# Sigmoid attention and FFN: float32 scores of unsplit q and k in the first three batches, and a decode without GpSimd

## The chip, the cores and the metric

The kernel runs on one core of one Trainium2 chip. The metric is the device time of one execution in microseconds; lower is better. The engines are named as in the profile: PE is TensorE (matmuls), PEld its weight loads, DVE is VectorE, ACT is ScalarE, POOL is GpSimd, SP is the queue that issues most DMAs.

## The reference

Two parts follow each other. Attention with a sigmoid in the place of the softmax, for 8 batches, 12 heads, 448 positions and a head dimension of 64, all float32:

```
scores = scale * np.matmul(q, k.transpose(0, 1, 3, 2)) - np.log(S)
attn = 1.0 / (1.0 + np.exp(-scores))
return np.matmul(attn, v).astype(np.float32)
```

Then a feed-forward network over the 3584 tokens (d_model 768, d_ff 2048). Its weights come as float64:

```
h = x @ w_in
g = 0.5 * h * (1.0 + erf(h * inv_sqrt2))
return (g @ w_out).astype(np.float32)
```

## The kernel before

**The split.** Most matmuls take operands of type `float32r`, which drop low bits. To keep the precision, an operand is split: ACT casts it to float32r (the high part), DVE subtracts that from the original (the low part), and PE sums three products, low by high, high by low, high by high. In FFN1 and FFN2 these are L450 to L452 and L497 to L499; each has 512 moving columns.

**Decoding.** `decoder()` (L92) turns the weights' float64 words into float32, once, in chunks of at most 384 columns (68 chunks; a unit is a block of w_in of 768 columns or of w_out of 1024). The chunk's raw words are loaded by SP (L118). `start` runs three DVE passes (L125 masks the exponent, L126 and L129 put the mantissa's bits together). `convert` runs two ACT passes over the exponent (L137, L140) and makes the mantissa a float32, on DVE (L142), or on ACT for chunks 24 to 39 (L146). `end` adds the sign on DVE (L154), and POOL multiplies mantissa and exponent (L163). The three steps of one chunk lie one step apart each. `decode(n)` (L187) advances this to step n; the calls are written out by hand between the other work, with the paces `PACE_A` and `PACE_F`: 20 steps in the first stage, 23 in FFN1 of block 0, the rest in the window behind it. Decoded units are stored to DRAM (scr_in by SP, scr_out by POOL's queue), and later blocks load them from there.

**Preparing.** `prepare_to` (L225) splits a unit for the matmuls: a cast on ACT (L237) and a subtraction on DVE (L238) into a tile `whl`. In block 0 there are two such tiles, so the cast for unit u+2 waits until PE is done with unit u. 

**Batches and blocks.** There are 8 batches and 7 FFN blocks of 512 tokens: a block has a batch's 448 tokens and 64 of the batch that was computed first (its results pass through DRAM, `scr_x`). The first three batches are "plain": the attention weights and v aren't split, and their product is a float32 matmul (`values_plain`, L364): 448 columns, with the two heads of a pair on the two halves of the array's columns (`pav[rows(j)]`), four chunks of keys, so eight matmuls a pair. Each float32 matmul shows as two records in the trace. For the fourth chunk of 64 keys both heads read rows 64 to 127.

The scores of all batches use split operands. `split_head` (L285) makes for each head `qs` (high part of q on the head's 64 rows, low part on the other 64; L292, L293), `ka` (cast of k, which the host has put on both row halves; L295, and a small subtraction L296) and `kb` (low part of k; L300). `scores` (L311) runs two matmuls for each chunk of 128 keys (L331, L332) and, in plain batches, two for the last 64 keys (L323, L324), and then three sigmoids on ACT (L355): 2 x 448 columns, 448 columns, and 448 on 64 rows. Behind the values, L373 (ACT) and L374 (DVE) split the result x; in the first batch SP stores it.

**The order of the work** is the order in which the code issues it, engine by engine (a manual schedule). `attention_first` (L410) computes two plain batches head by head. Then for each block `ffn1` and `window`; the window interleaves FFN2's matmuls with the attention of batch t+2, in equal shares. The third plain batch is in the window of block 0. PSUM: one score tile of two banks, four banks for values and single scores, two for the FFN.

Of the kernel before, what the change touches and what calls it, by code (L numbers as in the profile page):

```python
# [22 lines left out]
def tile_sigmoid_attention_gelu_ffn(  # L23
# [19 lines left out]
    CHUNKS = (0, 0), (1, 0), (1, 1), (0, 1)  # L43
# [14 lines left out]
    ps_f = ctx.enter_context(tc.tile_pool(name="ps_f", bufs=2, space=bass.MemoryType.PSUM))  # L58
# [17 lines left out]
    RING = 3  # L76
    PACE_A, PACE_F = 20, 23
    SUB = 384
    RAW = (("raw", RING), ("a", 2)), (("raw", RING), ("a", 2), ("ah", 3))
    EARLY, AHEAD = PACE_A + PACE_F - 3, 4  # L80
    WST = 3
    SHIFT, KEPT = 1, 4
    AHD = 3
    MLO, MHI = 24, 40
# [7 lines left out]
    def decoder():  # L92
# [3 lines left out]
            (kind, u, c0, min(SUB, width(kind) - c0))  # L96
            for kind, u in UNITS
            for c0 in range(0, width(kind), SUB)
        ]
        raws, parts, ended = {}, {}, [0]  # L100
        raw_ring = sb.tile([P, RING, 2 * SUB], U32, tag="raw", name="raw_ring", bufs=1)
        raw_next = itertools.cycle(range(RING))
        me_ring = sb.tile([P, RING, 2, SUB], U32, tag="me", name="me_ring", bufs=1)
        rings = [
            itertools.cycle([tag for n in range(4) for tag in ring if n < tag[1]]) for ring in RAW
        ]

        def load_to(n):
            for i in range(len(raws) + ended[0], min(n, len(chunks))):
                kind, u, c0, w = chunks[i]  # L110
                src = (w_in if kind == "in" else w_out)[u].rearrange("p a b -> p (a b)")
                tag, bufs = next(rings[i < EARLY])
                if tag == "raw":
                    raw = raw_ring[:, next(raw_next)]
                else:
                    raw = sb.tile([P, 2 * SUB], U32, tag=tag, name=f"raw{i}", bufs=bufs)
                raw = raw[:, : 2 * w]
                nc.sync.dma_start(raw.bitcast(I64), src[:, c0 : c0 + w])  # L118
                raws[i] = raw.rearrange("p (n t) -> p n t", t=2)

        def start(i):
            w = chunks[i][3]
            low, high = raws[i][:, :, 0], raws[i][:, :, 1]
            m, e = me_ring[:, i % RING, 0, :w], me_ring[:, i % RING, 1, :w]
            nc.vector.tensor_scalar(e, high, 0x7FF00000, None, op0=ALU.bitwise_and)  # L125
# [3 lines left out]
            nc.vector.scalar_tensor_tensor(  # L129
                m, low, 20, m, op0=ALU.logical_shift_right, op1=ALU.bitwise_or  # L130
            )
            parts[i] = m, e

        def convert(i):

            m, e = parts[i]
            nc.scalar.activation(  # L137
                e.bitcast(F32), e.bitcast(I32), AF.Relu, bias=1151.0 * 2**23, scale=-8.0
            )
            nc.scalar.activation(e, e.bitcast(F32), AF.Relu, bias=255.0 * 2**23, scale=-1.0)  # L140
            if not MLO <= i < MHI:
                nc.vector.tensor_scalar(  # L142
                    m.bitcast(F32), m.bitcast(I32), 2.0**-32, 1.5, op0=ALU.mult, op1=ALU.add
                )
            else:
                nc.scalar.activation(  # L146
                    m.bitcast(F32), m.bitcast(I32), AF.Identity, bias=1.5, scale=2.0**-32
                )

        def end(i):  # L150
            high = raws.pop(i)[:, :, 1]
            ended[0] += 1
# [10 lines left out]
            nc.gpsimd.tensor_tensor(t, m.bitcast(F32), e.bitcast(F32), op=ALU.mult)  # L163
# [12 lines left out]

    class Weights:
# [9 lines left out]
        def decode(self, n):  # L187

            while self.steps < n:
# [18 lines left out]
        def load_to(self, n):  # L208

            while self.loaded < min(n, len(self.units)):  # L210
                i = self.loaded
                b, kind, u = self.units[i]
                while self.decoded < min(i + 1, len(UNITS)):
                    self.decode(self.steps + 1)
# [45 lines left out]
    def load_pair(b, hp):  # L260
        b, h = there(b, 2 * hp)
        hp = h // 2
# [5 lines left out]
        if b == 0 and hp == 0:  # L268
            for j in range(2):
                nc.sync.dma_start(kr[:, j], k[(b - 1) % B, hp, :, j])  # L270
        else:
            nc.sync.dma_start(kr, k[(b - 1) % B, hp])
        raws[b, hp] = qr, kr

    def load_v(b, hp):
        b, h = there(b, 2 * hp)
        hp = h // 2
        if b >= B or hp >= NPAIR:
            return
        tag = ("vr", "vs")[hp % 2] if b < PLAIN else "vr"  # L280
        vr = sb.tile([P, 2, 4, D], F32, tag=tag, name=f"vr{b}_{hp}")
# [3 lines left out]
    def split_head(b, h):  # L285
        b, h = there(b, h)
        if b >= B or h >= NH:
# [3 lines left out]
        qs = sb.tile([P, S], F32R, tag="qs", name=f"qs{b}_{h}", bufs=3)  # L291
        nc.scalar.copy(qs[rows(j)], qr[rows(j)])  # L292
        nc.vector.tensor_tensor(qs[rows(1 - j)], qr[rows(j)], qs[rows(j)], op=ALU.subtract)  # L293
        ka = sb.tile([P, S + TAIL], F32R, tag="ka", name=f"ka{b}_{h}", bufs=3)
        nc.scalar.copy(ka[:, :S], kr[:, j])  # L295
# [15 lines left out]
    def scores(b, h):  # L311
        plain = b < PLAIN
        qs, ka, kb = heads.pop((b, h))
        a = []
        for t in range(2):
            tag = ("al", ("wst", "wst", "ah")[b])[t] if plain else "a"
            bufs = {"wst": WST, "a": 2}.get(tag, 3)
            a.append(sb.tile([P, 2, S], F32, tag=tag, name=f"a{b}_{h}_{t}", bufs=bufs))
# [3 lines left out]
        if plain:  # L322
            nc.tensor.matmul(last[:D], ka[:, S - TAIL : S], qs, start=True, stop=False)  # L323
            nc.tensor.matmul(last[:D], ka[:, S:], qs, start=False, stop=True)  # L324
        else:

            nc.tensor.matmul(last, ka[:, S - TAIL :], qs, start=True, stop=True)
        for c in range(3):
            keys = slice(c * P, c * P + P)
            o = sc0 if c == 0 else sc1[:, c - 1]  # L330
            nc.tensor.matmul(o, ka[:, keys], qs, start=True, stop=False)  # L331
            nc.tensor.matmul(o, kb[:, keys], qs, start=False, stop=True)  # L332
        tail = a[0][D:, 1]
        if not plain:
            nc.scalar.copy(tail, last[:D])
            nc.vector.tensor_tensor(tail, last[D:], tail, op=ALU.add)
# [243 lines left out]
```

## Time and profile before

| | us |
|---|---|
| median of 3 runs | 1276.54 (1274.54 to 1277.57) |
| the profiled execution | 1277.24 |
| its span in the trace | 1275.5 |
| first FFN1 matmul of block 0 | 112.3 |
| first FFN2 matmul of block 0 | 195.7 |
| first FFN1 matmul of block 1 | 315.95 |

The page gives busy time and idle time by engine and by group of instructions. A group's row has the line of the code, the engine, the operation, the tiles (out<-in) with their shapes, the count, then busy us and mean ns of one, then the idle time of the engine just before them and what ended it. Matmuls are pipelined: a record lasts longer than the step from one to the next, so PE's pace is read from start to start. A window's row has the length and each engine's busy time (with the count of instructions), the granted clock, the DMA share and GB/s.

### The profile page before, as it was taken

To read this page: it belongs to the slowest core of one execution; us is meant where nothing else is said; L and a number is where in the kernel's file an instruction comes from. 1 tells how busy PE (TensorE), PEld (TensorE's weight loads), DVE (VectorE), ACT (ScalarE), POOL (GpSimd) and SP (SyncE) were. 2 spreads that over 40 slices of the span, in tenths; PEclk is the share of its full clock that TensorE was granted. 3 is DMA by queue.
4 is the path that set the end of the run, shared out by engine and by line. 5 is a ranking of instruction groups with operands and counts; after the bars stand their busy time and mean duration, and the time that the engine had idled before them with its cause. 6 is when DMAs were issued, how large, how long until landed. Compare 5 with 4: busy or idle time off the path is not lost.

```text
span 1275.5 us, 15676 instructions
## 1 busy us (share of the span) xinstructions
PE 1229.8 (96%) x5448; PEld 985.9 (77%) x5448; DVE 826.7 (65%) x1359; ACT 872.2 (68%) x1427; POOL 89.1 (7%) x84
## 2 busy tenths in 40 slices
PE   7889888989999999999999999999999999999998
PEld 4445665756888888888888888888888888888887
DVE  5776888883458973479844798436985458863420
ACT  7987677764459984499844898547995469964421
POOL 1111333441000000000000000000000000000000
PEclk9999898999999999999999999999999999999999
DMA  7764756652445323554225442254422444323330
GB/s 284 233 213 127 219 185 191 204 183 88 153 143 168 113 67 102 164 158 149 66 84 167 155 143 70 91 159 150 151 75 82 156 154 139 109 66 99 116 123 34
DMA packets 83775, 176.41 MB, mean 138 GB/s; under 512 B 24432, under 2 KB 37744, under 8 KB 83696
## 3 DMA queue, kind: packets, MB, share of 16 engines
q1 hardware_dynamic: 81968, 169.12, 41.8%
q0 software_dynamic: 1728, 6.29, 1.2%
q8 instruction: 43, 0.70, 0.2%
q14 instruction: 36, 0.29, 0.1%
HBM read 149.03 MB, written 26.35 MB: 137 GB/s over the span
## 4 chain that ended last, share of the span: by engine, by line
PE 80%; DVE 7%; ACT 5%; DMA 2%; issue 2%; POOL 2%; SPq 0%; DVEq 0%; POOLq 0%; ACTq 0%
PE po L497 11%; PE po L498 11%; PE po L499 11%; PE ph L450 10%; PE ph L451 10%; PE ph L452 10%; PE pav L398 7%; PE sc L331 4%; PE sc L332 4%; ACT a L355 2%; PE pav L364 2%; POOL w_out L163 2%; DVE me_ring L154 1%; DVE whl L238 1%; DMA scr_in<-w_in 1%
## 5 line engine op out<-in xcount | busy, mean ns | idle before, releaser
L450 PE MATMUL ph<-xh,whl 128*128 128x512 f32 x672 | 263.9, 393 | 10.3 <-DVE whl L238 10.3
L497 PE MATMUL po<-g,whl 128*128 128x512 f32 x672 | 264.0, 393 | 9.5 <-DVE whl L238 9.5
L498 PE MATMUL po<-g,whl 128*128 128x512 f32 x672 | 262.9, 391 | 0.0
L499 PE MATMUL po<-g,whl 128*128 128x512 f32 x672 | 262.8, 391 | 0.0
L451 PE MATMUL ph<-xl,whl 128*128 128x512 f32 x672 | 262.8, 391 | 0.0
L452 PE MATMUL ph<-xh,whl 128*128 128x512 f32 x672 | 262.6, 391 | 0.0
L238 DVE TENSOR_TENSOR whl<-wst,whl 128x768 fp32r<-128x768 f32 (+1 forms) x168 | 179.5, 1072 | 66.8 <-ACT whl L237 63.6
L467 DVE TENSOR_TENSOR g<-gf,g 128x512 fp32r<-128x512 f32 x112 | 77.8, 695 | 213.2 <-ACT g L466 213.2
L465 ACT ACTIVATE gf<-ph 128x512 f32<-128x512 f32 x112 | 66.8, 597 | 205.1 <-PE ph L452 190.9
L450 PEld LDWEIGHTS ph<-xh,whl 128*128 128x128 f32 x672 | 126.9, 189 | 40.3 <-DVE whl L238 13.3
L237 ACT CAST whl<-wst 128x768 fp32r<-128x768 f32 (+1 forms) x168 | 155.4, 928 | 2.2 <-PE po L499 0.8
L497 PEld LDWEIGHTS po<-g,whl 128*128 128x128 f32 x672 | 126.6, 188 | 38.8 <-DVE whl L238 11.6
L355 ACT ACTIVATE a<-sc 128x896 f32<-128x896 f32 x192 | 129.6, 728 | 28.3 <-PE sc L332 24.0
L499 PEld LDWEIGHTS po<-g,whl 128*128 128x128 f32 x672 | 126.6, 188 | 27.1
L452 PEld LDWEIGHTS ph<-xh,whl 128*128 128x128 f32 x672 | 127.0, 189 | 26.6
L451 PEld LDWEIGHTS ph<-xl,whl 128*128 128x128 f32 x672 | 127.0, 189 | 26.2
L498 PEld LDWEIGHTS po<-g,whl 128*128 128x128 f32 x672 | 126.6, 188 | 23.8
L331 PE MATMUL sc<-qs,ka 128*128 128x448 f32 x288 | 108.6, 377 | 14.9 <-ACT a L355 13.6
L348 DVE TENSOR_TENSOR al<-a,ah 128x896 fp32r<-128x896 f32 x120 | 97.8, 854 | 34.8 <-ACT ah L347 34.8
L332 PE MATMUL sc<-qs,kb 128*128 128x448 f32 x288 | 107.4, 373 | 0.0
L293 DVE TENSOR_TENSOR qs<-qr,qs 64x448 fp32r<-64x448 f32 x96 | 62.0, 646 | 45.8 <-ACT qs L292 43.9
L347 ACT CAST ah<-a 128x896 fp32r<-128x896 f32 x120 | 85.6, 753 | 6.1 <-PE pav L398 4.6
(62 smaller groups left out, 1514.6 us busy)
## 6 DMA issues: line engine op xcount, KB each, us to landing
wst<-scr_in SPq DMA_DIRECT2D x96, 384.0 KB, 3.1
wst<-scr_out SPq DMA_DIRECT2D x72, 512.0 KB, 3.2
kr<-k_dram SPq DMA_DIRECT2D x47, 448.0 KB, 4.4
vr<-v_dram SPq DMA_DIRECT2D x48, 256.0 KB, 3.9
qr<-q_dram SPq DMA_DIRECT2D x48, 224.0 KB, 3.2
out_dram<-ob SPq DMA_DIRECT2D x42, 224.0 KB, 2.0
raw<-w_in_dram SPq DMA_DIRECT2D x20, 384.0 KB, 4.2
scr_in<-w_in SPq DMA_DIRECT2D x16, 384.0 KB, 4.3
```

Of the source, the lines that this page charges most:

```text
L237: nc.scalar.copy(hl[:, 0, :w], t[:, :w])
L238: nc.vector.tensor_tensor(hl[:, 1, :w], t[:, :w], hl[:, 0, :w], op=ALU.subtract)
L331: nc.tensor.matmul(o, ka[:, keys], qs, start=True, stop=False)
L332: nc.tensor.matmul(o, kb[:, keys], qs, start=False, stop=True)
L348: nc.vector.tensor_tensor(al[t][:, c], a[t][:, c], ah[t][:, c], op=ALU.subtract)
L355: nc.scalar.activation(a, sc, AF.Sigmoid, bias=NEG_LOG_S, scale=SCALE)
L450: nc.tensor.matmul(ph, wl, xh[:, cc], start=cc == 0, stop=False)
L451: nc.tensor.matmul(ph, wh, xl[:, cc], start=False, stop=False)
L452: nc.tensor.matmul(ph, wh, xh[:, cc], start=False, stop=cc == NC - 1)
L497: nc.tensor.matmul(po, wl, g[fc][:, 0], start=first, stop=False)
L498: nc.tensor.matmul(po, wh, g[fc][:, 1], start=False, stop=False)
L499: nc.tensor.matmul(po, wh, g[fc][:, 0], start=False, stop=last)
```

## The change

The first part concerns the scores of the three plain batches. q and k are no longer split: for each pair of heads and chunk of keys there are two float32 matmuls of 64 rows, head 0 on rows 0 to 63 and head 1 on rows 64 to 127. They write to two banks of one tile, and one sigmoid takes both (2 x 448 columns). For the last 64 keys the two heads write the two partition halves of one bank, and one sigmoid takes both on 128 rows. In the values of that chunk head 0 now reads rows 0 to 63. The work goes pair by pair and chunk by chunk, loads come three pairs ahead, and k is loaded for each head on its half only. During the first stage a second score tile of two banks exists; the FFN's banks are allotted behind that stage.

```diff
+    def scores_plain(n, c):
+        qr, kr, _ = raws[n]
+        keys = slice(c * P, min(c * P + P, S))
+        if c < 3:
+            pool = next(score_pools)
+            sc = pool.tile([P, 2, 512], F32, tag="sc", name=f"sc{n}_{c}")[:, :, :S]
...
+        for j in range(2):
+            o = sc[:, j] if c < 3 else sc[rows(j)]
+            nc.tensor.matmul(o, kr[rows(j), keys], qr[rows(j)], start=True, stop=True)
+        sigmoid(a, sc)
...
+    def values_plain(n):
+        for c in range(4):
+            a = attn.pop((n, c))
             for j in range(2):
-                r = slice(0, P) if c < 3 else slice(D, P)
+                r = slice(0, P) if c < 3 else rows(j)
                 nc.tensor.matmul(
-                    pav[rows(j), :S], vr[r, j, c], a[j][t][r, n], start=c == 0, stop=c == 3
+                    pav[rows(j), :S], vr[r, j, c], a[:, j] if c < 3 else a[r],
+                    start=c == 0, stop=c == 3,
                 )
...
     def attention_first():
+        total = 2 * NPAIR
+        load_plain(0)
+        load_plain(1)
+        W.decode(0)
+        load_plain(2)
+        for n in range(total):
+            for c in range(4):
+                scores_plain(n, c)
+                if c == 1 and n > 0:
+                    values_plain(n - 1)
+                W.decode(PACE_A * (4 * n + c + 1) / (4 * total))
+            load_plain(n + 3)
+            if n == NPAIR + 2:
                 load_tokens(0)
+            W.prepare_to(min(n - total + 3, 2))
+        values_plain(total - 1)
```

The second part is the decode. Chunks are a whole unit of w_in (768 columns) or half a unit of w_out (512), 40 in all. The mantissa stays an integer, and the last DVE pass scales it and multiplies it by the exponent; L142, L146 and POOL's L163 are gone. A chunk takes two steps: three DVE passes; then the two ACT passes, and behind them the last two DVE passes of the chunk before and the load of the chunk after next. The paces are 14 chunks in the first stage, 8 in FFN1 of block 0 and up to 22 in the window. Three raw buffers and two pairs of mantissa and exponent remain.

```diff
-    PACE_A, PACE_F = 20, 23
-    SUB = 384
+    PACE_A, PACE_F, PACE_W = 14, 8, 22
+    SUB_IN, SUB_OUT = NC * P, NFH * P // 2
...
             nc.vector.tensor_scalar(
-                m, high, 12, 0x80000000, op0=ALU.logical_shift_left, op1=ALU.bitwise_xor
+                m, high, 11, 0x80000000, op0=ALU.logical_shift_left, op1=ALU.bitwise_or
             )
             nc.vector.scalar_tensor_tensor(
-                m, low, 20, m, op0=ALU.logical_shift_right, op1=ALU.bitwise_or
+                m, low, 21, m, op0=ALU.logical_shift_right, op1=ALU.bitwise_or
             )
...
-            nc.gpsimd.tensor_tensor(t, m.bitcast(F32), e.bitcast(F32), op=ALU.mult)
+            nc.vector.scalar_tensor_tensor(
+                t, m, 2.0**-31, e.bitcast(F32), op0=ALU.mult, op1=ALU.mult
+            )
...
+        for i in range(len(chunks) + 1):
+            if i == 0:
+                load(2)
             if i < len(chunks):
                 start(i)
+                yield False
+                scale(i)
+            if i > 0:
+                end(i - 1)
+                load(i + 2)
```

In FFN1 of block 0 the prepare of the unit after next stands ahead of the two gelus instead of behind them:

```diff
             ph = hidden(b, fc, range(NC - 1, NC))
+            if b == 0:
+                W.prepare_to(W.pos[b, "in", fc] + 3)
             g[fc] = g_tile(fc, f"g{b}_{fc}")
```

In the window of block 0 a chunk of scores comes before each of 24 equal shares of FFN2's work, and the values of the pair before come behind the share of chunk 1:

```diff
+        if att < PLAIN:
+            for n in range(att * NPAIR, (att + 1) * NPAIR):
+                for c in range(4):
+                    share = (4 * (n % NPAIR) + c + 1) / (4 * NPAIR)
+                    scores_plain(n, c)
+                    W.decode(PACE_A + PACE_F + PACE_W * (share - 1 / (8 * NPAIR)))
+                    until(share)
+                    if c == 1 and n % NPAIR:
+                        values_plain(n - 1)
+                    W.decode(PACE_A + PACE_F + PACE_W * share)
+                load_plain(n + 3)
+            values_plain(n)
```

The later batches compute as before, with fewer buffers: `qs` has two instead of three, `ka` and `kb` are one tile `ks` with two instead of three each, and the two `a` tiles of a head are one tile.

More of the change, by code (lines that the diff above doesn't have):

```diff
@@ L95, in decoder, with load @@
         chunks = [
-            (kind, u, c0, min(SUB, width(kind) - c0))
+            (kind, u, c0, sub)
             for kind, u in UNITS
-            for c0 in range(0, width(kind), SUB)
-        ]
[L100 to L119, printed above, removed]
+            for sub in (SUB_IN if kind == "in" else SUB_OUT,)
+            for c0 in range(0, width(kind), sub)
+        ]
+        raws, parts = {}, {}
+        raw_ring = sb.tile([P, 2, 2 * SUB], U32, tag="raw", name="raw_ring", bufs=1)
+        me_ring = sb.tile([P, 2, 2, SUB], U32, tag="me", name="me_ring", bufs=1)
+        def load(i):
+            if i >= len(chunks):
+                return
+            kind, u, c0, w = chunks[i]
+            src = (w_in if kind == "in" else w_out)[u].rearrange("p a b -> p (a b)")
+            if i % 3 < 2:
+                raw = raw_ring[:, i % 3]
+            else:
+                raw = sb.tile([P, 2 * SUB], U32, tag="a", name=f"raw{i}", bufs=1)
+            raw = raw[:, : 2 * w]
+            nc.sync.dma_start(raw.bitcast(I64), src[:, c0 : c0 + w])
+            raws[i] = raw.rearrange("p (n t) -> p n t", t=2)
         def start(i):
@@ L187, in decode @@
         def decode(self, n):
-            while self.steps < n:
+            while self.steps < 2 * n:
                 if next(self.decoder, False):
@@ L213, in load_to @@
                 while self.decoded < min(i + 1, len(UNITS)):
-                    self.decode(self.steps + 1)
+                    self.decode((self.steps + 1) / 2)
                 if b == 0:
@@ L267, in load_pair @@
         nc.sync.dma_start(qr, q[(b - 1) % B, hp])
[L268 to L272, printed above, removed]
-        raws[b, hp] = qr, kr
[L275 to L281, printed above, removed]
+        nc.sync.dma_start(kr, k[(b - 1) % B, hp])
+        raws[b, hp] = qr, kr
+        vr = sb.tile([P, 2, 4, D], F32, tag="vr", name=f"vr{b}_{hp}")
         nc.sync.dma_start(vr, v[(b - 1) % B, hp])
@@ L285, in split_head @@
     def split_head(b, h):
-        b, h = there(b, h)
         if b >= B or h >= NH:
@@ L311, in scores @@
     def scores(b, h):
[L312 to L318, printed above, removed]
+        qs, ks = heads.pop((b, h))
+        at = sb.tile([P, 2, 2, S], F32, tag="a", name=f"a{b}_{h}", bufs=1)
+        a = [at[:, 0], at[:, 1]]
         last = ps_av.tile([P, 512], F32, tag="pav", name=f"sc{b}_{h}_l")[:, :S]
@@ L339, in scores @@
         split_head(b, h + 2)
-        sigmoid(tail, last[:D] if plain else tail)
-        if not plain:
-            ah, al = [], []
-            for t in range(2):
-                ah.append(sb.tile([P, 2, S], F32R, tag="ah", name=f"ah{b}_{h}_{t}", bufs=3))
-                al.append(sb.tile([P, 2, S], F32R, tag="al", name=f"al{b}_{h}_{t}", bufs=3))
-            for t, c in (1, slice(0, 2)), (0, 0):
-                nc.scalar.copy(ah[t][:, c], a[t][:, c])
-                nc.vector.tensor_tensor(al[t][:, c], a[t][:, c], ah[t][:, c], op=ALU.subtract)
-            nc.scalar.copy(ah[0][D:, 1], a[0][D:, 1])
-            nc.vector.tensor_tensor(ah[0][:D, 1], a[0][D:, 1], ah[0][D:, 1], op=ALU.subtract)
-            a = list(zip(ah, al))
@@ L352, in scores @@
-        attn[b, h] = a
+        sigmoid(tail, tail)
+        ah, al = [], []
+        for t in range(2):
+            ah.append(sb.tile([P, 2, S], F32R, tag="ah", name=f"ah{b}_{h}_{t}", bufs=3))
+            al.append(sb.tile([P, 2, S], F32R, tag="al", name=f"al{b}_{h}_{t}", bufs=3))
+        for t, c in (1, slice(0, 2)), (0, 0):
+            nc.scalar.copy(ah[t][:, c], a[t][:, c])
+            nc.vector.tensor_tensor(al[t][:, c], a[t][:, c], ah[t][:, c], op=ALU.subtract)
+        nc.scalar.copy(ah[0][D:, 1], a[0][D:, 1])
```

199 lines of the change are left out of this document (79 added, 120 removed).

## The prediction

> **What bounds the kernel now.** I read the page first, for the span; then the busy time by windows, cut where the first FFN1 matmul (L450), the first FFN2 matmul (L497) and the next FFN1 begin:
>
> ```profile
> span 1275.5 us, 15676 instructions
> ```
> ```profile
> core 0: us, PE busy (x) PEld busy (x) DVE busy (x) ACT busy (x) POOL busy (x), PEclk, DMA share, GB/s
> 0.00:112.30 112.30, 92.39 (x384) 46.44 (x384) 76.19 (x178) 95.08 (x171) 17.35 (x21) 0.95 0.68 228
> 112.30:195.70 83.40, 72.72 (x299) 57.24 (x297) 71.27 (x129) 59.23 (x113) 27.22 (x24) 0.96 0.58 181
> 195.70:315.95 120.25, 109.12 (x473) 75.74 (x473) 87.58 (x190) 77.12 (x136) 44.53 (x39) 0.97 0.54 170
> 315.95:381.00 65.05, 65.05 (x288) 53.88 (x287) 28.77 (x36) 32.94 (x53) 0.00 (x0) 1.00 0.46 145
> ```
>
> The four rows are: A, attention of the two first plain batches (12 head pairs); B, FFN1 of block 0; C, FFN2 of block 0 with the third plain batch (6 pairs); and FFN1 of block 1, where nothing is decoded. In A ScalarE (ACT) is busy 95.08 of 112.30 us, so A is an ACT stage. In B the same 288 matmuls that need 65.05 us in block 1 take 83.40, beside 27.22 us of GpSimd (POOL) and 71.27 of VectorE (DVE). C contains the same count of FFN matmuls (65.05) and has the decoding too. From 315.95 on PE is full (65.05 busy of 65.05 in the last row), and the change leaves the work there as it is; I leave those 959.55 us alone. (The merged and shortened buffers of split heads, `a` and `qs`, are rewritten only after the matmuls or subtractions that the same engine order already waits for; I cost that at nothing, and at about 0.1 us per head, 6 us in all, if a wait does appear.)
>
> What ACT and DVE do in A, per instruction, and what the shorter decode chunks cost (last three rows, whole run):
>
> ```profile
> L355 ACT ACTIVATE a<-sc 128x896 f32<-128x896 f32 x24 | 21.8, 910 | 4.7 <-PE sc L332 4.7
> L295 ACT CAST ka<-kr 128x448 fp32r<-128x448 f32 x24 | 13.6, 567 | 0.6 <-DMA kr<-k_dram 0.3
> L292 ACT CAST qs<-qr 64x448 fp32r<-64x448 f32 x24 | 13.5, 560 | 1.5 <-DMA qr<-q_dram 1.2
> L355 ACT ACTIVATE a<-sc 128x448 f32<-128x448 f32 x24 | 12.9, 539 | 0.0
> L355 ACT ACTIVATE a<-sc_l 64x448 f32<-64x448 f32 x24 | 12.9, 537 | 0.6
> L137 ACT ACTIVATE me_ring<-me_ring 128x384 f32<-128x384 int32 x18 | 9.4, 524 | 2.8 <-DVE me_ring L125 2.4
> L374 DVE TENSOR_TENSOR xl<-pav,xh 128x448 fp32r<-128x448 f32 x11 | 6.8, 621 | 2.9 <-ACT xh L373 2.9
> L129 DVE SCALAR_TENSOR_TENSOR me_ring<-raw,me_ring 128x384 uint32<-128x384 uint32 x12 | 6.7, 559 | 0.4
> L373 ACT CAST xh<-pav 128x448 fp32r<-128x448 f32 x11 | 5.8, 523 | 2.9 <-PE pav L364 2.9
> L125 DVE TENSOR_SCALAR me_ring<-raw 128x384 uint32<-128x384 uint32 x12 | 4.2, 353 | 0.0
> ```
> ```profile
> L137 ACT ACTIVATE me_ring<-me_ring 128x256 f32<-128x256 int32 x12 | 5.0, 417 | 18.4 <-DVE me_ring L125 18.4
> L129 DVE SCALAR_TENSOR_TENSOR me_ring<-raw_ring,me_ring 128x256 uint32<-128x256 uint32 x6 | 2.6, 426 | 0.2
> L125 DVE TENSOR_SCALAR me_ring<-raw_ring 128x256 uint32<-128x256 uint32 x6 | 1.8, 295 | 3.0 <-POOL w_out L163 2.8
> ```
>
> **The decode, per chunk.** Between 256 and 384 columns ACT grows by (524-417)/128 = 0.84 ns a column, a two-input DVE pass by 1.04, a one-input DVE pass by 0.45. So a w_in chunk of 768 costs DVE 2 x 0.53 + 3 x 0.96 = 3.9 us and ACT 2 x 0.85 = 1.7 us; a w_out chunk of 512 costs 2.9 and 1.3. POOL's multiply goes. Per weight column DVE pays about what it paid; what goes is the collision that the next rows show.
>
> **A, on ACT.** Removed: the two casts per head (L292, L295), 1.13 us. A pair's sigmoids fall from 2 x (910+539+537) to 3 x 910 + 539 = 3.27 us. With L373 (0.52) and 14 chunks over 12 pairs (1.97) ACT has 5.8 us a pair; DVE has 14/12 x 3.9 + 0.62 = 5.2. Before, ACT's 95.08 us were 7.9 a pair.
>
> **A, on PE.** All float32 products that the trace has are those of the values (L364), two heads on two column halves:
>
> ```profile
> 296.13 0.39 PE L499 MATMUL po<-g,whl 128*128 128x512 f32 x1
> 296.45 3.38 PE L364 MATMUL pav<-a,vr 128*64 128x448 f32 x16
> 299.76 0.50 PE L497 MATMUL po<-g,whl 128*128 128x512 f32 x1
> 300.10 0.39 PE L498 MATMUL po<-g,whl 128*128 128x512 f32 x1
> ...
> 303.02 0.36 PE L331 MATMUL sc<-qs,ka 128*128 128x448 f32 x1
> 303.22 0.37 PE L332 MATMUL sc<-qs,kb 128*128 128x448 f32 x1
> ```
> ```profile
> 297.26 0.14 PEld L364 LDWEIGHTS pav<-a,vr 128*64 128x64 f32 x2 [0.23 <-issue]
> 297.63 0.14 PEld L364 LDWEIGHTS pav<-a,vr 128*64 128x64 f32 x2 [0.23 <-issue]
> 298.01 0.14 PEld L364 LDWEIGHTS pav<-a,vr 128*64 128x64 f32 x2 [0.23 <-issue]
> 298.86 0.19 PEld L364 LDWEIGHTS pav<-a,vr 64*64 64x64 f32 x4 [0.70 <-issue]
> ```
>
> Eight products make 16 records, two loads every 0.375 us, so two float32 products of two heads take 0.75 us and a pair's values 3.0. The block occupies 296.36 (where the next FFN matmul would have stood, 65.05/288 = 0.226 after 296.13) to 299.76, 3.40 us, and the matmul behind it starts its successor 0.34 rather than 0.226 us later: 0.51 us of changing shapes, of which 0.10 is the change to 64 rows inside it (298.01 plus two steps is 298.76; it came at 298.86).
>
> No run here has float32 products on two row halves. Below, a chunk of scores cannot cost less than 0.75, the column halves' price, since it has the same columns and records; above, 1.5, if the halves take turns. I take 0.75: the nearest row is the column pair. Then a pair has 4 x 0.75 = 3.0 us of scores, where the split products cost 16 x 0.20 (303.02 to 303.22) = 3.2: PE gains nothing, it only no longer waits for splits. That with A's values makes 6.0 us a pair, and five changes of shape at 0.10 to 0.20, 0.75: 6.75. ACT (5.8) is close below, and where its two decode passes (1.7) stand ahead of the third sigmoid they hold PE about 0.8 us, for 4 of 14 chunks, 0.25 a pair: 7.0.
>
> The Trainium skill (TensorE: Matmul & The Clock Gate, "Measured speedup vs the span model") gives 3.07 times for four row tiles; if two lose as large a share, a chunk is 0.98 (an estimate from that page) and the sum below 16 us higher. No run here shows row tiles, so the sum keeps 0.75.
>
> **A, the start.**
>
> ```profile
> 4.79 0.61 PE L323 MATMUL sc_l<-qs,ka 128*64 128x448 f32 x1 [4.79 <-DVE qs L293]
> 7.99 0.36 DVE L125 TENSOR_SCALAR me_ring<-raw_ring 128x384 uint32<-128x384 uint32 x1 [1.24 <-DMA raw_ring<-w_in_dram]
> 8.55 0.57 PE L331 MATMUL sc<-qs,ka 128*128 128x448 f32 x1
> 10.00:20.00 10.00, 8.80 (x38) 4.51 (x38) 6.94 (x18) 9.74 (x19) 1.01 (x1) 1.00 1.02 395
> ```
>
> Without splits the first product can start near 4.1 instead of 4.79, at the slow early rate (0.57 against 0.36 us). But the first raw chunk, now 768 KB and queued behind two pairs of q, k, v (1.4 MB), lands near 11 us at up to 395 GB/s, not 7.99; ACT's first decode pass stands ahead of the third sigmoid of pair 0 and waits for it, and PE waits for that sigmoid's bank. So pair 2 begins near 20 us. A = 20 + 10 x 7.0 + 3.5 (last values) = 94 us, 86 to 102: the low end with shape changes at nothing, the high end with a period of 7.8 through ACT. Each SP queue entry (a raw load behind a decode's end, the x stores behind L373 and L374) is issued within its pair, and loads are three pairs ahead; 16 raw chunks of 0.79 MB, 15 pairs of 0.72 and 3 MB of x make 26 MB, 280 GB/s over 94 us, under 395.
>
> **B.**
>
> ```profile
> L450 PE MATMUL ph<-xh,whl 128*128 128x512 f32 x96 | 39.8, 415 | 10.3 <-DVE whl L238 10.3
> L238 DVE TENSOR_TENSOR whl<-w_in,whl 128x768 fp32r<-128x768 f32 x14 | 23.1, 1647 | 0.0
> ```
> ```profile
> L238 DVE TENSOR_TENSOR whl<-wst,whl 128x768 fp32r<-128x768 f32 x96 | 91.9, 958 | 20.1 <-ACT whl L237 17.5
> L467 DVE TENSOR_TENSOR g<-gf,g 128x512 fp32r<-128x512 f32 x112 | 77.8, 695 | 213.2 <-ACT g L466 213.2
> ```
>
> PE waits for L238, and L238 takes 1647 ns here against 958 later, where POOL has nothing: a subtraction beside POOL's multiplies is 0.7 us longer. In the change B has 8 chunks (2 of w_in, 6 of w_out halves: 25 us of DVE) instead of 23 of 384 columns, and no POOL. DVE needs 16 x (0.96 + 0.70) + 25 = 52 of 65 us. The prepare that now stands ahead of the two gelus makes them, and L467 behind them, wait for one cast of 768 columns, about the 0.85 us of a decode pass of that width, within a unit of 65.05/16 = 4.1 us; the next unit's weights are there by then, so I cost it at nothing (at 16 x 0.85 = 14 us if that lead were gone). So PE becomes the bound: 65.05 + 1.5 = 66.5 (65 to 69).
>
> **C.**
>
> ```profile
> L238 DVE TENSOR_TENSOR whl<-w_out,whl 128x1024 fp32r<-128x1024 f32 x11 | 13.9, 1267 | 0.3 <-ACT whl L237 0.3
> ```
>
> FFN2 65.05; values 6 x 3.51; 24 score chunks, each alone between FFN matmuls, 0.75 + 0.41 (the block's 0.51 less the 0.10 inside) = 1.16, together 27.8; waits 2: 116 (111 with changes of shape at half that, 120 with waits of 6, over half of what L450 has in B now). That is only 4 us under 120.25: the scores here are dearer for PE than the 16 x 0.2 they replace, and what pays is that the decode stops holding L238. DVE has the rest of the decode (18 chunks of 2.9, 53 us), L238's 13.9 and 6 x 0.62 for the values: 71 of 116.
>
> **Sum.** 94 + 66.5 + 116 = 276.5 against 315.95: 39.5 less. The profiled execution took 1277.24 us, 1.74 over its span, and the median is 0.7 below it: 1275.5 - 39.5 + 1.74 - 0.7 = 1237 us. The three ranges give 262 to 291, thus 1222 to 1252.
>
> **Rivals.** (1) *The row halves take turns.* Then each of 72 chunks costs 0.75 more, 54 us: A 130, C 134, in all 1291, slower than before. It decides from 0.54 us more a chunk (39.5/72), a chunk of 1.3 us. For it: nothing in the trace overlaps on rows. Against: the same instruction overlaps on columns, and 64-row products (298.86) run at the full step. Chance 0.10. The Trainium skill (TensorEngine Tiling (Array Packing), "Theoretical Speedup") has up to 2 times for 64 rows, against this rival; no trace here shows it.
>
> (2) *Only the tail's halves take turns*: the fourth chunk of scores and of values lies for both heads in one PSUM bank, and comes from different rows for the first time (before, both heads used rows 64 to 127). 18 pairs x 2 x 0.75 = 27 us: 1264. Against: at 298.86 two heads share a bank without loss. Chance 0.07. This is what the Trainium skill says under "Gotcha 1: PSUM Pressure" of TensorEngine Tiling (Array Packing): row tiles cannot use one bank at once; no row tile stands in this trace.
>
> (3) *A stays an ACT stage*: ACT's order makes PE and ACT wait by turns, and a pair takes 7.9 us as now. A is 20 + 79 + 3.5 = 103, in all 1246. For it: 5.8 of 7.0 is a high load for an engine in order. Chance 0.13.
>
> **How the numbers follow.** My forecast has 0.70. The range 1222 to 1256 holds it and rival 3, and leaves out rivals 1 and 2 and a little beyond. About 0.2% (2.5 us) is what a measurement of this kernel can tell from no change. Faster 0.88 (forecast, 2 and 3), slower 0.10 (rival 1), within 0.02 (half-overlapping halves near 1.3 us).
>
> **What would show it.** Right: the first FFN1 matmul near 94 us and the first of FFN2 near 160; score products in pairs with two loads per 0.375 us; L238 near 958 ns in B; POOL nearly empty; no PE wait for L238 in B; the last 959 us as before. Wrong: score products 0.75 us apart within a chunk (rival 1), only the tail's (2), or long PE idle before score chunks released by the sigmoid in all of A (3); a stretch after 276 us that is longer than 959.5 would mean the shared buffers do cost something.

## The result and the profile after

The changed kernel takes 1243.53 us (median of 4 runs, 1241.04 to 1244.74), the kernel before 1276.88 beside it: a ratio of 0.9739, 95% interval 0.9719 to 0.9760, so 33.4 us less. Forecast were 1237 us and 39.5 less. The profiled execution took 1242.82 us with a span of 1241.0.

Lines have moved: the score products of plain batches are L347, their sigmoid L313, their values L359 and the split of x L369 and L370; the split of weights is L225 (ACT) and L226 (DVE), the decode L116 to L146, FFN1 L432 to L434, FFN2 L481 to L483. The busy time by windows of the kernel after, cut at the first FFN1 matmul, at the first score of the window (it comes just before the first FFN2 matmul) and at block 1:

```profile
core 0: us, PE busy (x) PEld busy (x) DVE busy (x) ACT busy (x) POOL busy (x), PEclk, DMA share, GB/s
0.00:96.07 96.07, 87.84 (x384) 27.25 (x384) 59.06 (x82) 66.95 (x91) 0.20 (x4) 0.98 0.83 266
96.07:161.60 65.53, 65.53 (x290) 53.98 (x289) 48.10 (x70) 38.35 (x61) 1.20 (x2) 1.00 0.54 185
161.60:281.79 120.19, 115.15 (x482) 65.44 (x481) 70.67 (x114) 61.65 (x88) 5.89 (x10) 0.99 0.49 161
281.79:1241.00 959.21, 955.52 (x4297) 806.31 (x4295) 591.69 (x863) 640.45 (x1007) 0.00 (x0) 1.00 0.37 120
```

The two middle stages of the kernel before, cut in the same way:

```profile
112.30:193.49 81.19, 70.89 (x290) 55.93 (x289) 69.09 (x127) 57.89 (x110) 26.19 (x24) 0.96 0.59 182
193.49:315.95 122.46, 110.95 (x482) 77.06 (x480) 89.76 (x192) 78.45 (x140) 45.56 (x40) 0.97 0.54 169
```

So A (attention) went from 112.30 to 96.07, B (FFN1) from 81.19 to 65.53, C (the window) from 122.46 to 120.19, and the rest, 959.55 before, is 959.21. ACT is no longer the engine of A: 66.95 busy of 96.07. B is at its floor, PE busy throughout. C hardly moved, although POOL's 45.56 us are gone; that is the gap in this result, and the experiments go there.

### The profile page after: what moved, and what is told of

Its sections match the earlier page's. It is cut to its first block, busy times and chain, and to the rows that moved or that the text cites. A ratio compares the mean times of both kernels' runs of the same rounds, so it can differ in the third digit from the quotient of the medians.

```text
span 1241.0 us, 15043 instructions
## 1 busy us (share of the span) xinstructions
PE 1224.0 (99%) x5448; PEld 953.0 (77%) x5448; DVE 769.5 (62%) x1127; ACT 807.4 (65%) x1247; POOL 7.3 (1%) x16
## 4 chain that ended last, share of the span: by engine, by line
PE 96%; ACT 2%; DMA 1%; SPq 0%; issue 0%; DVE 0%; ACTq 0%; DVEq 0%
PE po L481 13%; PE ph L432 12%; PE ph L434 12%; PE ph L433 12%; PE po L482 12%; PE po L483 12%; PE pav L390 7%; PE sc L293 6%; PE pav L359 5%; PE sc L347 3%; PE sc_l L347 1%; PE sc_l L288 1%; DMA raw_ring<-w_in_dram 1%; ACT a L313 0%; ACT me_ring L132 0%; DMA raw_ring<-w_out_dram 0%
## 5 line engine op out<-in xcount | busy, mean ns | idle before, releaser
L481 PE MATMUL po<-g,whl 128*128 128x512 f32 x672 | 265.4, 395 | 0.0
L483 PE MATMUL po<-g,whl 128*128 128x512 f32 x672 | 262.4, 391 | 0.0
L432 PE MATMUL ph<-xh,whl 128*128 128x512 f32 x672 | 261.5, 389 | 0.0
L434 PE MATMUL ph<-xh,whl 128*128 128x512 f32 x672 | 261.4, 389 | 0.0
L226 DVE TENSOR_TENSOR whl<-wst,whl 128x768 fp32r<-128x768 f32 (+1 forms) x168 | 179.6, 1072 | 66.2 <-ACT whl L225 63.1
L481 PEld LDWEIGHTS po<-g,whl 128*128 128x128 f32 x672 | 126.4, 188 | 40.0 <-issue 17.2
L225 ACT CAST whl<-wst 128x768 fp32r<-128x768 f32 (+1 forms) x168 | 155.4, 928 | 1.3
L313 ACT ACTIVATE a<-sc 128x896 f32<-128x896 f32 (+1 forms) x174 | 129.8, 787 | 29.0 <-PE sc L347 19.9
L483 PEld LDWEIGHTS po<-g,whl 128*128 128x128 f32 x672 | 126.4, 188 | 27.3
L432 PEld LDWEIGHTS ph<-xh,whl 128*128 128x128 f32 x672 | 126.1, 188 | 26.8 <-issue 0.7
L434 PEld LDWEIGHTS ph<-xh,whl 128*128 128x128 f32 x672 | 126.1, 188 | 26.2
L390 PE MATMUL pav<-ah,vs 128*128 128x448 f32 x240 | 87.7, 365 | 0.0
L293 PE MATMUL sc<-qs,ks 128*128 128x448 f32 x360 | 82.9, 366 | 0.0
L293 PEld LDWEIGHTS sc<-qs,ks 128*128 128x128 f32 x360 | 67.6, 188 | 6.8
```

Of the source, the lines that this page charges most:

```text
L225: nc.scalar.copy(hl[:, 0, :w], t[:, :w])
L226: nc.vector.tensor_tensor(hl[:, 1, :w], t[:, :w], hl[:, 0, :w], op=ALU.subtract)
L293: nc.tensor.matmul(o, ks[:, keys], qs, start=n == 0, stop=n == 1)
L313: nc.scalar.activation(a, sc, AF.Sigmoid, bias=NEG_LOG_S, scale=SCALE)
L390: nc.tensor.matmul(pav[:, :S], vs[:, j, c], a, start=n == 0, stop=n == len(terms) - 1)
L432: nc.tensor.matmul(ph, wl, xh[:, cc], start=cc == 0, stop=False)
```

## The experiments

A, B, C and the rest of each run's profiled execution, in us, cut as above. Times are medians of four or five runs, that of one_half is one run; a median can differ by some us from the profiled execution that the stages come from. The kernel before had medians of 1275.94 to 1276.12 beside them.

| run | A | B | C | rest | time |
|---|---|---|---|---|---|
| before | 112.3 | 81.2 | 122.5 | 959.6 | 1276.88 |
| after | 96.1 | 65.5 | 120.2 | 959.2 | 1243.53 |
| one_half | 124.0 | 65.5 | 132.1 | 959.2 | 1282.59 |
| pool_back | 98.2 | 65.5 | 123.0 | 959.3 | 1246.16 |
| old_no_pool | 110.4 | 74.1 | 110.4 | 959.5 | 1256.55 |
| prepare_behind | 95.0 | 65.5 | 121.6 | 959.3 | 1244.02 |
| late_decode | 90.5 | 65.5 | 123.0 | 959.2 | 1238.47 |
| pace_28 | 95.3 | 65.5 | 116.6 | 959.3 | 1238.01 |
| tail_third | 101.1 | 65.5 | 116.7 | 959.2 | 1247.96 |
| all_three | 97.5 | 65.5 | 117.1 | 959.2 | 1241.10 |
| start_and_pace | 90.3 | 65.5 | 117.4 | 959.2 | 1234.90 |
| split_in_window | 98.2 | 65.4 | 111.1 | 959.6 | 1234.68 |
| split_start_pace | 91.4 | 65.4 | 117.6 | 959.6 | 1234.58 |
| split_late_decode | 90.5 | 65.4 | 111.7 | 959.6 | 1228.40 |

**Do the two row halves overlap?** (one_half)

```diff
-            nc.tensor.matmul(o, kr[rows(j), keys], qr[rows(j)], start=True, stop=True)
+            nc.tensor.matmul(o, kr[rows(0), keys], qr[rows(0)], start=True, stop=True)
```

> Both heads' score products take their operands from rows 0 to 63, so head 1's scores are those of head 0 computed again; counts and shapes stay. Theory (the two row halves run at the same time, a float32 product of 448 columns takes 0.75 us): each of the 72 chunks costs 0.75 us more, 54 us in all; first FFN1 matmul near 130 us instead of 96, the whole 1290 to 1300 us. Rival (nothing overlaps, a product simply takes 0.375 us wherever it lies, so that the halves had no part in the result): chunk steps as they are, 1243 us.

Weight loads of the kernel after: start, duration, and how many were merged into the row.

```profile
43.70 0.30 PEld L347 LDWEIGHTS sc<-qr,kr 64*128 64x128 f32 x4 [0.70 <-issue]
44.18 0.19 PEld L347 LDWEIGHTS sc<-qr,kr 64*128 64x128 f32 x2 [0.18 <-issue]
44.55 0.19 PEld L347 LDWEIGHTS sc<-qr,kr 64*128 64x128 f32 x2 [0.18 <-issue]
```

The same in one_half:

```profile
36.17 0.29 PEld L347 LDWEIGHTS sc<-qr,kr 64*128 64x128 f32 x2 [0.70 <-issue]
36.66 0.19 PEld L347 LDWEIGHTS sc<-qr,kr 64*128 64x128 f32 x1 [0.19 <-issue]
37.03 0.19 PEld L347 LDWEIGHTS sc<-qr,kr 64*128 64x128 f32 x1 [0.19 <-issue]
37.87 0.19 PEld L347 LDWEIGHTS sc_l<-qr,kr 64*64 64x64 f32 x4 [0.65 <-issue]
```

On two halves, two loads every 0.375 us; on one half, one every 0.375. The halves run at the same time, and two cost what one costs. The tail's load (64 x 64, four at once at 37.87) kept its pace, since its two products still go to two column halves; I had forgotten that. So 54 of the 72 chunks are 0.75 us longer, 40.5 us, and measured are 39 (27.9 in A, 11.9 in C of the profiled execution). In A the values of two neighbouring pairs start 9.10 us apart (32.87 to 41.97) instead of 6.86, three times 0.75 more. The theory is right, its 54 us a miscount. The Trainium skill (TensorE: Matmul & The Clock Gate, "Measured speedup vs the span model") has 3.07 times for four row tiles; the estimate of 0.98 us a chunk that I drew from it doesn't hold here, two tiles lose nothing.

**What is GpSimd's multiply worth?** (pool_back undoes it in the kernel after; old_no_pool does it alone in the kernel before)

```diff
-            nc.vector.scalar_tensor_tensor(
-                t, m, 2.0**-31, e.bitcast(F32), op0=ALU.mult, op1=ALU.mult
-            )
+            nc.vector.tensor_scalar(m.bitcast(F32), m, 2.0**-31, None, op0=ALU.mult)
+            nc.gpsimd.tensor_tensor(t, m.bitcast(F32), e.bitcast(F32), op=ALU.mult)
```

> The changed kernel with the last multiply of the decode on GpSimd again, and a one-input VectorE pass ahead of it that makes the mantissa a float32. Theory (GpSimd's multiplies hold VectorE's subtraction of prepared weights): that subtraction, 0.959 us for every w_in unit in FFN1 of block 0, is 1.3 to 1.7 us for those that meet a multiply; VectorE has 17 us to spare there, so most of it stays hidden: FFN1 of block 0 takes 65.5 to 68 us, the window 1 to 4 us more, the whole 1244 to 1250 us. Rival (the gain in FFN1 came from the paces alone, 8 chunks there in place of 23 smaller ones): subtractions stay at 0.96 us, 1243 us.

```diff
-            if not MLO <= i < MHI:
...
-            nc.gpsimd.tensor_tensor(t, m.bitcast(F32), e.bitcast(F32), op=ALU.mult)
+            nc.vector.scalar_tensor_tensor(
+                t, m, 2.0**-31, e.bitcast(F32), op0=ALU.mult, op1=ALU.mult
+            )
```

> The kernel before, scores, chunks and paces as they were, but the decode's last multiply on VectorE (scaling the integer mantissa in the same pass), so GpSimd does no arithmetic. Theory (the collision with GpSimd is what FFN1 of block 0 waited for): prepared-weight subtractions there fall from 1.65 to 0.96 us, VectorE's sum in that stage is 65 to 72 us, the stage 70 to 74 us instead of 81; the first attention stage stays at 112 us, since ScalarE sets it; the window 118 to 121; the whole 1263 to 1269 us. Rival (VectorE's load as such is the limit, and the extra passes cost what the collision costs): 1275 to 1280 us.

The subtraction of prepared weights in B, in the kernel after, in pool_back and in old_no_pool:

```profile
L226 DVE TENSOR_TENSOR whl<-w_in,whl 128x768 fp32r<-128x768 f32 x15 | 14.4, 958 | 15.1 <-ACT whl L225 15.1
```
```profile
L225 DVE TENSOR_TENSOR whl<-w_in,whl 128x768 fp32r<-128x768 f32 x15 | 19.2, 1282 | 13.0 <-ACT whl L224 13.0
```
```profile
L232 DVE TENSOR_TENSOR whl<-w_in,whl 128x768 fp32r<-128x768 f32 x14 | 13.3, 952 | 0.1
```

With POOL idle it takes 0.95 us in every kernel, with POOL's multiplies in the stage 1.28 on average or, before, 1.65. The Trainium skill (SBUF — State Buffer, "Who interferes with whom") says that a VectorE instruction with two SBUF inputs contends with a GpSimd instruction that reads SBUF, and that the ports they share are an exclusive lock; the trace agrees: in the kernel before, a multiply runs from 128.97 to 130.35, and the subtraction that starts at 129.41 ends at 131.16, 0.81 us behind the multiply's end. In pool_back B still takes 65.5 us, because the new paces leave DVE 16 us free there. So the change's gain in B can't be put down to the collision alone: with the new paces B is at its floor with POOL multiplying too. In all pool_back costs 2.6 us (1246.16, a ratio of 0.9765, 0.9747 to 0.9782), as expected; its profile has two long waits for the sigmoid (5.04 us at the start, 4.93 in C) where the kernel after has 3.40 and 2.74. In the old kernel the same removal is worth far more (there the edit also drops the pass that made the mantissa a float32, on DVE, or on ACT for 16 chunks). The windows of old_no_pool:

```profile
110.40:184.53 74.13, 67.59 (x291) 53.57 (x290) 69.32 (x143) 51.53 (x95) 1.20 (x2) 1.00 0.61 200
184.53:294.90 110.37, 107.30 (x481) 75.77 (x480) 88.70 (x193) 77.25 (x139) 5.31 (x10) 1.00 0.60 186
```

The ratio to before is 0.9848 (0.9829 to 0.9867), 19.4 us, more than I expected. B's 74.13 is in line with what was expected (DVE is busy 69.32 of it). The miss is C: 110.37, where 118 to 121 were expected. The subtraction of prepared weights itself gained little there, it only fell from 1.27 to 1.22 us; but DVE comes to it earlier, and PE's waits for it fell from 9.5 to 2.1 us. Other rows of C show where DVE had lost its time, first in the kernel before, then in old_no_pool:

```profile
L296 DVE TENSOR_TENSOR ka<-kr,ka 128x64 fp32r<-128x64 f32 x11 | 8.7, 793 | 0.2
L125 DVE TENSOR_SCALAR me_ring<-raw_ring 128x384 uint32<-128x384 uint32 x11 | 3.9, 356 | 8.3 <-POOL w_out L163 8.3
```
```profile
L290 DVE TENSOR_TENSOR ka<-kr,ka 128x64 fp32r<-128x64 f32 x11 | 2.5, 226 | 0.2
L125 DVE TENSOR_SCALAR me_ring<-raw_ring 128x384 uint32<-128x384 uint32 x11 | 4.0, 360 | 0.2
```

A small subtraction of the split of k took 793 ns beside POOL and takes 226 without; and DVE no longer waits for POOL's multiply to give back the buffer of mantissa and exponent. Part of the gain is the clock: it was 0.96 in B and 0.97 in C before, and is 1.00 in both here, which is worth about 3 us a stage (0.04 x 81, 0.03 x 122). With its split scores, C of old_no_pool is 10 us shorter than the 120.19 of the kernel after; so it seems that the scores of the change make the window longer and hid what the decode gave there. That is tried below (split_in_window).

**The prepare ahead of the gelus** (prepare_behind: the call for the unit after next stands behind them again)

> The changed kernel with the preparation of the unit after next behind the two gelus again. Theory (it was costed at nothing, since the unit is needed 4 us later): FFN1 of block 0 65.5 us, the whole within 1.5 us of 1243.5. Rival (the lead matters): matmuls wait for the subtraction, up to 14 us more. The other way is possible too: without the cast ahead of the gelus, the first sigmoid of the window comes about 1 us earlier, and the wait of 2.3 us that PE has there gets 1 us shorter.

1244.02 (0.9748, 0.9731 to 0.9764) against 1243.53, B 65.53 in both: worth nothing either way, as costed. PE's wait of 2.30 us at the start of the window stays 2.30, so the other way is out too.

**The waits of A and C.** In the kernel after, instructions in order of time around the start:

```profile
10.36 1.02 PE L347 MATMUL sc<-qk 64*128 64x448 f32 x4
11.61 0.56 DVE L116 TENSOR_SCALAR me_ring<-raw_ring 128x768 uint32<-128x768 uint32 x1 [10.74 <-DMA raw_ring<-w_in_dram]
12.21 0.85 ACT L129 ACTIVATE me_ring<-me_ring 128x768 f32<-128x768 int32 x1 [3.22 <-DVE me_ring L116]
13.84 0.90 ACT L313 ACTIVATE a<-sc 128x896 f32<-128x896 f32 x1
14.79 1.02 PE L347 MATMUL sc<-qk 64*128 64x448 f32 x4 [3.40 <-ACT a L313]
15.74 5.07 PE L359 MATMUL pav<-a,vr 128*64 128x448 f32 x16
```

The raw weights land at 11.61; ACT's decode pass waits for them, the third sigmoid (13.84) stands behind it, and PE needs that sigmoid's bank. The values behind the wait last 5.07 us instead of 3.38. In C there are two such waits, of 2.30 us at 167.21 (the first sigmoid of the window stands behind the gelus, a decode and an ACT_TABLE_LOAD of 1.28 us) and this one:

```profile
237.98 1.05 ACT L225 CAST whl<-w_out 128x1024 fp32r<-128x1024 f32 x1
238.93 0.64 ACT L129 ACTIVATE me_ring<-me_ring 128x512 f32<-128x512 int32 x1
241.65 0.43 DVE L116 TENSOR_SCALAR me_ring<-raw 128x512 uint32<-128x512 uint32 x1
242.11 0.63 ACT L129 ACTIVATE me_ring<-me_ring 128x512 f32<-128x512 int32 x1 [1.89 <-DVE me_ring L116]
245.49 0.43 DVE L116 TENSOR_SCALAR me_ring<-raw_ring 128x512 uint32<-128x512 uint32 x1 [1.02 <-DMA raw_ring<-w_out_dram]
245.95 0.63 ACT L129 ACTIVATE me_ring<-me_ring 128x512 f32<-128x512 int32 x1 [2.54 <-DVE me_ring L116]
247.15 0.90 ACT L313 ACTIVATE a<-sc 128x896 f32<-128x896 f32 x1
248.10 1.57 PE L347 MATMUL sc<-qk 64*128 64x448 f32 x4 [2.74 <-ACT a L313]
```

The cast at 237.98 is that of the tenth of the twelve w_out units. Behind it `prepare_to` asks that the unit two further on, the last, be there (`load_to`, which decodes what is missing), and at this place, about two thirds into the window, a pace of 22 has three chunks to go. They are issued at one stroke: three decode passes (L129) on ACT and no sigmoid between them. The second and the third wait 1.89 and 2.54 us for DVE's first pass over their chunk; ahead of it DVE has the rest of the chunk before and the subtraction, and of the third's wait 1.02 us are the raw chunk's DMA. The clock granted behind both waits, in the kernel after:

```profile
14.70:20.70 6.00, 5.92 (x20) 1.55 (x20) 1.39 (x2) 2.08 (x4) 0.00 (x0) 0.72 0.61 189
248.10:251.90 3.80, 3.80 (x10) 2.13 (x11) 2.04 (x4) 1.29 (x2) 0.53 (x1) 0.55 0.23 95
```

0.72 over 6.0 us and 0.55 over 3.8: each of these two waits is followed by slow matmuls that cost some 1.7 us. Not every wait is: behind the 2.30 us before 167.21 the clock stayed at 1.00.

The decode steps of the first stage four chunks later (late_decode):

```diff
-                W.decode(PACE_A * (4 * n + c + 1) / (4 * total))
+                W.decode(PACE_A * (4 * n + c - 3) / (4 * total - 4))
```

> The changed kernel with the decode steps of the first stage four chunks of scores later, so that none stands between the sigmoids of pair 0. Theory (the start is 2.6 us longer than forecast because ScalarE's first decode pass waits for the raw weights' DMA at 11.6 us ahead of the third sigmoid): PE's wait of 3.4 us before 14.79 us goes, and with it the slow clock of the 5 us of values behind it; the first FFN1 matmul comes 3 to 5 us earlier than at 96.07, the whole 1238.5 to 1241 us. Rival (the start is bound by the DMAs of the first pairs or by the clock's warming up): less than 1 us.

A higher pace in the window (pace_28):

```diff
-    PACE_A, PACE_F, PACE_W = 14, 8, 22
+    PACE_A, PACE_F, PACE_W = 14, 8, 28
```

> The changed kernel with PACE_W 28 in place of 22: all units are decoded by about two thirds of the window of block 0. Theory (the wait of 2.74 us before 248.10 us and the slow matmuls behind it come from three chunks decoded at one stroke, since the load of block 1's first unit asks that all be decoded): that wait goes, the window is 3 to 4.5 us shorter, the whole 1239 to 1241 us. Rival (a late raw load as such holds the sigmoid, whatever the pace): as many waits, spread, 1243 us or more.

```profile
PE sc L347 <- ACT a L313: 1.0, 4, 0.3
```
```profile
PE sc L347 <- ACT a L313: 3.0, 3, 2.3
```

These are PE's waits for the sigmoid (total, times, longest) in A of late_decode and in C of pace_28: the long one of the start is gone, and in C only the 2.3 is left of length. late_decode takes 1238.47 (0.9705, 0.9689 to 0.9720; A 90.5), pace_28 1238.01 (0.9706, 0.9688 to 0.9725; C 116.6). Both waits went as the theories had it, and both rivals are out; the gains are a little over what was expected (the first FFN1 matmul comes 5.6 us earlier instead of 3 to 5, pace_28 is 1 us under its range). What asks for the decode is the last unit of block 0, though, not the first of block 1 as I had written. That C is 123.0 in late_decode's profile is the clock: behind its waits of 2.30 and 2.80 us it was 0.51 for 3.5 and for 6.9 us. start_and_pace puts both together:

> The changed kernel with the later decode steps of the first stage and PACE_W 28, without the new chunk order. Theory (two separate waits, each with its own cause, and the chunk order is what held back the three edits together): the gains of 5.1 and 5.5 us add, 1232 to 1235 us. Rival (the pace and the start share a cause, ScalarE's order): 1237 to 1240 us.

1234.90 (0.9679, 0.9666 to 0.9692), in the theory's range: 8.6 of the 10.6 us.

**The changes of shape** (tail_third: the order of the chunks is 0, 1, 3, 2 in both stages)

```diff
-            for c in range(4):
+            for i, c in enumerate((0, 1, 3, 2)):
```

> The changed kernel with the chunks of scores in the order 0, 1, 3, 2: the tail chunk (64 x 64 shapes) directly behind the values, whose last products have the same shape. Theory (each change of shape costs PE 0.15 to 0.2 us and PE sets the first stage): one to two changes fewer for each of 17 pairs, a pair's period of 6.86 falls to 6.5 to 6.7 us, the first FFN1 matmul comes 2 to 4 us earlier, the whole 1239 to 1242 us. Rival (the steps between shapes are waits for ScalarE or latencies, not the change itself): 1243 us.

A pair's PE rows in the kernel after:

```profile
31.68 3.38 PE L359 MATMUL pav<-a,vr 128*64 128x448 f32 x16
34.98 1.02 PE L347 MATMUL sc<-qk 64*128 64x448 f32 x4
35.94 0.97 PE L347 MATMUL sc_l<-qk 64*64 64x448 f32 x4
36.84 1.77 PE L347 MATMUL sc<-qk 64*128 64x448 f32 x8
38.54 3.38 PE L359 MATMUL pav<-a,vr 128*64 128x448 f32 x16
```

and in tail_third:

```profile
36.93 3.38 PE L359 MATMUL pav<-a,vr 128*64 128x448 f32 x16
40.13 0.92 PE L347 MATMUL sc_l<-qk 64*64 64x448 f32 x4
40.98 1.02 PE L347 MATMUL sc<-qk 64*128 64x448 f32 x4
41.84 0.92 PE L347 MATMUL sc<-qr,kr 64*128 64x448 f32 x4
44.62 1.02 PE L347 MATMUL sc<-qr,kr 64*128 64x448 f32 x4 [1.86 <-ACT a L313]
```
```profile
PE sc L347 <- ACT a L313: 12.0, 11, 2.8
```

The step from the values to the next scores fell from 3.30 to 3.20, the two chunks behind it took 0.85 and 0.86 instead of 0.96 and 0.90: together 0.25 us less, so changes of shape do cost PE. And chunk 2 now stands right ahead of the next pair's chunk 0, so that chunk 1 of that pair finds its bank still waiting for chunk 2's sigmoid: 12.0 us of waits in A. In all 1247.96 (0.9777, 0.9755 to 0.9799), slower than the kernel after. (The profiled execution took 1244.26 us, the other three 1247.11 to 1250.64; what they lost beyond it isn't known.) Neither theory had that; the order of the chunks sets how long a sigmoid has before its bank is wanted. The three edits together:

> The three edits together: later decode steps in the first stage, PACE_W 28, and chunk order 0, 1, 3, 2. Theory (three separate causes): the gains add, 8 to 12 us, 1231 to 1236 us. Rival (each wait that goes uncovers another on ScalarE): 1237 to 1241 us.

1241.10 (0.9725, 0.9711 to 0.9740): the upper end of the rival's range, but for this reason; without the chunk order it is start_and_pace, 6.2 us faster.

**Split scores in the window.** The third plain batch takes its scores from split q and k, as in the kernel before, and that batch's loads, sigmoids and values go with them; A and the decode stay as changed.

```diff
-                    scores_plain(n, c)
+                scores_split(att, h)
...
+        nc.tensor.matmul(last[:D], ks[:, S - TAIL : S], qs, start=True, stop=False)
+        nc.tensor.matmul(last[:D], ks[:, S : S + TAIL], qs, start=False, stop=True)
```

split_in_window, this alone:

> The changed kernel, but the third plain batch, in the window of block 0, takes its scores from split operands again (16 split products a pair at 0.2 us, no change of shape); the first two batches and the decode stay as changed. Theory (in the window PE is the bound, and a lone chunk of float32 products costs it 1.15 us where four split products cost 0.82): 65.05 of FFN2, 12 x 8 x 0.204 = 19.6 of scores, 21.1 of values and 2 to 4 of waits make a window of 108 to 110 us instead of 120.2; the whole 1231 to 1234 us. Rival (the casts and subtractions of the split, 18 us of VectorE and 13 of ScalarE, return as waits beside the decode): window 115 us or more, 1238 us or more.

split_start_pace, with the later decode steps and a pace of 28:

> All that helped together: split scores in the window, later decode steps in the first stage, PACE_W 28. Theory (separate causes): first stage 90.5, FFN1 65.5, window 106 to 109, the whole 1225 to 1228 us. Rival (with 28 the decode crowds the splits on VectorE): window 112 or more, 1230 us or more.

split_late_decode, with the later decode steps and a pace of 22:

> Split scores in the window and the later decode steps of the first stage, with PACE_W at 22 as in the changed kernel. Theory (with splits VectorE is the engine that the pace of 28 overloads in the window; with 22 it isn't): window 109 to 112 us as with 22 before, first stage 90 to 92, the whole 1226 to 1230 us. Rival (the window's 117.55 us with a pace of 28 came from the earlier start, which shifts the loads against each other): window 115 us or more, 1233 us or more.

split_in_window takes 1234.68 (0.9678, 0.9665 to 0.9691), 0.7 us over its range; C fell from 120.2 to 111.1, 1 us over the range, and A began with a wait of 5.77 us, the longest at that place. Against pace_28, whose C has no 2.74 us wait either, the split scores are worth 5.5 us of C, not 9. With both other edits nothing is gained (1234.58): C is 117.6. There PE waits for prepared weights:

```profile
PE po L517 <- DVE whl L226: 7.3, 3, 3.8
```

This is what the rival said: ahead of the first of these waits, from 163.4 to 175.3 us DVE works with a pause of 0.93 us, mostly on decode passes, before it comes to the subtraction that PE waits for until 176.62. With the same start and a pace of 22, C is 111.7 again, so it is the pace and not the earlier start. split_late_decode takes 1228.40 (0.9627, 0.9614 to 0.9640), as its theory had it. Its windows:

```profile
0.00:90.50 90.50, 85.30 (x385) 27.04 (x385) 59.10 (x82) 66.64 (x91) 0.20 (x4) 1.00 0.85 265
90.50:155.89 65.39, 65.39 (x290) 54.06 (x289) 49.05 (x73) 40.38 (x65) 1.20 (x2) 1.00 0.60 205
155.89:267.57 111.68, 108.36 (x481) 76.81 (x480) 84.01 (x147) 74.86 (x120) 5.70 (x10) 0.98 0.58 187
```

This is the fastest version here, 15 us under the change and 48 under the kernel before.

## Why the prediction was right

The direction and the size hold, 39.5 us were forecast, 33.4 measured, inside the range; the mechanism holds for A, and for B and C with the reservations below. By its steps:

- **Row halves at 0.75 us a chunk**: right, and shown by one_half. Rival 1 is out. Rival 2, the tail's halves in one bank, is out too: the tail's step is 0.90 us (35.94 to 36.84), no longer than the 0.96 of a full chunk, and the step from the values, whose last chunk is of that form too, to the next scores is 3.30 (31.68 to 34.98). The Trainium skill (TensorEngine Tiling (Array Packing), "Gotcha 1: PSUM Pressure") says that row tiles cannot use one bank at once; for two tiles that write different partitions of the bank this trace differs.
- **A's period**: 7.0 us forecast, 6.86 between 31.68 and 38.54, and 7.02 on average from pair 2 to pair 11 (22.59 to 92.77). Five changes of shape at 0.15 on average: (6.86 - 6.0)/5 = 0.17. Rival 3 is out, ACT is idle for 29 of 96 us.
- **A's start**: pair 2 at 20 forecast, at 22.59 measured; that is all of A's error (94 against 96.07). The wait was foreseen with its cause, the raw chunk at 11 against 11.61; the slow clock behind it was not in the sum.
- **B**: 66.5 forecast, 65.5 measured. Cut as in the prediction, at the first FFN2 matmul (162.55), B is 66.5 and C 119.2. The collision that B was put down to is real, but pool_back shows that the new paces were enough for B.
- **C**: the mis-sized term, 116 forecast, 120.2 measured. The shape term is right: a lone chunk was put at 1.16 us, and the rows give 1.15, from 161.51, where the next FFN matmul was due, to 162.55, plus 0.11 in the step behind it:

```profile
161.28 0.39 PE L434 MATMUL ph<-xh,whl 128*128 128x512 f32 x1
161.60 1.02 PE L347 MATMUL sc<-qk 64*128 64x448 f32 x4
162.55 0.50 PE L481 MATMUL po<-g,whl 128*128 128x512 f32 x1
162.89 0.39 PE L482 MATMUL po<-g,whl 128*128 128x512 f32 x1
```

  The waits were put at 2 us; they are 2.30 + 2.74, and 1.7 of slow clock. With these the terms make 65.05 + 21.1 + 24 x 1.15 + 5.04 + 1.7 = 120.5 against 120.2, so these terms account for C. pace_28 takes the second wait away.
- **The rest**: 959.21 against 959.55, the shared buffers cost nothing.
- **The median**: of the 6.5 us that it is over the forecast, 5.3 are in the three stages; some 1.4 are that it lies 0.7 above the profiled execution, where 0.7 below was taken over from the kernel before.

What the prediction said of C in passing, that the scores there are dearer than what they replace, turned out to be the largest loss in the change: split scores give 9 us back (split_in_window), 5.5 where the 2.74 us wait is gone anyway. Of the 33.4 us, 19.4 come from the decode without POOL if it is made alone (old_no_pool); between the profiles of old_no_pool and of the kernel after, the new scores, chunks and paces give 14.3 in A and 8.6 in B, and take 9.8 in C.

What stays open: A of kernels that differ only behind A, or not at all in the start's order, ranges from 95.0 to 98.2 us, with waits at the start between 3.4 and 5.8 us. The traces show the landing of the first raw weights vary with it: 10.63 and 10.93 us with A at 95.0 and 95.3 (prepare_behind, pace_28), 11.61 with 96.1 (after), 12.62 and 13.07 with 98.2 (pool_back, split_in_window). Why it varies is open.

## What to carry to other kernels

Price a matmul of another shape with its surroundings: the same float32 chunk costs 0.75 to 0.95 us in a run of its like and 1.15 alone between other matmuls, so that it paid in one stage and lost in the other. When an engine off the critical path is slow only beside another engine, look for a shared resource; and try the lighter pace by itself, as it alone was enough for B here (pool_back). And before moving an instruction ahead, count how long each buffer's reader then has until the buffer is wanted.

## What the runs showed of the hardware

- Two float32 products with 64 rows each, on the two row halves of the array, run at the same time: two loads per 0.375 us against one when both use the same half.
- A change of the array's shape costs PE about 0.17 us between float32 products (a pair's period of 6.86 less 6.0 of products, over five changes).
- After a wait of 2.74 us the clock granted to PE was 0.55 for 3.8 us, after one of 3.40 us 0.72 for 6.0 us; the Trainium skill (TensorE: Matmul & The Clock Gate, "HAM oscillation — how this bites in real kernels") puts the limit at gaps of about 3.4 us, and here shorter ones were enough at times: 2.30 us in late_decode (0.51 for 3.5 us behind it). But behind the same 2.30 us in the kernel after, and behind 2.76 us in tail_third, the clock stayed at 1.00.
